# Gated S4 convolution and MLP on one core: the last group of the turn loaded in two parts, its rows reseated

## The chip, the cores and the metric

The kernel runs on one core of one Trainium2 chip. The metric is the device time of the program in microseconds (us): the median of the runs before is 535.32 us (three runs, 534.39 to 537.9). One execution was profiled; it took 536.27 us itself, of which 534.5 us are the span from the first to the last instruction. All times "at" which something happens below are counted from the start of that span.

## The reference

Every token of a sequence of L = 2048 rows and D = 512 columns goes through two branches, which a sigmoid gate mixes.

```
g = sigmoid((x * gate_w).sum(-1, keepdims=True))       # one gate per row
# branch a: S4 convolution, x is [1, 2048, 512], 128 states per column
dt = exp(log_dt)[:, None];  A = A_re + 1j*A_im;  dB = dt * (B_re + 1j*B_im)
P  = exp((dt * A)[:, :, None] * arange(L))
K  = einsum("dn,dnl,dn->dl", C, P, dB).real            # taps, 512 x 2048
y  = irfft(rfft(pad(x^T)) * rfft(pad(K)))[..., :L]     # causal convolution by FFT of 4096
a  = y^T + x * Dskip
# branch b: MLP with F = 1792
h  = gelu(x @ w1 + b1);  b = h @ w2 + b2
return g * a + (1 - g) * b
```

## The kernel before, in words

The kernel has two stages. The first one, `front`, makes the taps K, the first half of the transforms of the signal and of the taps, and almost all of the MLP. Its order on the engines is worked out ahead by a planner from costs and due times. It leaves the MLP's part of the result in the output tensor in DRAM, and the half transforms in the DRAM tensors `tu_d` and `tk_d`. The change does not touch it, apart from a table of constants that it does not use.

The second stage, `conv`, is written out by hand, in the order in which each engine runs it. It works on 32 frequencies n of the outer transform, two at a time in 16 steps s:

- `fetch` and `load_u` bring the half transforms of frequency n back from DRAM (SP's queue), eight frequencies ahead for the taps.
- `signal`, `taps` and `product` do the second half of the forward transforms on TensorE (L1090), copy the taps out on ScalarE (L1098), and multiply on VectorE (L1112 to L1117).
- `inverse` does the first half of the inverse transform on TensorE (L1129), into the PSUM tiles `pa`, one for each frequency: 128 partitions, which stand for 32 values of q, two of i and two of c (c is real or imaginary), by 512 columns.
- `turn` copies `pa` to an SBUF tile `sa` on ScalarE (L1135), and stores it in the DRAM tensor `t4_d` (L1138; the profile calls the tensor t_d). Eight frequencies form a group; there are four groups g. Behind the last store of a group, `turn` loads the group from `t4_d` into the SBUF tile `t3` (L1147; the profile calls the tile t). That is the turn: in `sa` the frequencies lie in different tiles and q lies on the partitions, and in `t3` frequency, i and c lie on the 128 partitions and 32 q by 512 columns lie in a row of 64 KB. One frequency of a group owns four partitions, and a group owns 32.

The first three groups are loaded by the GpSimd queue, in four DMAs of 512 KB, each with 32 rows of 16 KB. The last group, behind frequency 31, is on the path to the end: its last store goes out on ScalarE's queue, and its eight loads of 256 KB, each with 32 rows of 8 KB (four of the 32 q), go out alternately on ScalarE's and SP's queue. Each of the eight waits until all eight stores of the group have landed, so the one that landed last lets them go.

Between the last `inverse` and the first use of `t3`, TensorE works off the remainder of the MLP that `front` put aside for this place (`rest`, L1168 to L1170), and one matmul that keeps it busy (`warm`, L1206).

The final loop over m = 0..7 does the second half of the inverse transform: for m, four of the 32 q of `t3` (4m to 4m+3, on all partitions) are multiplied by the constant `g1t` into two PSUM tiles `pb` (L1218). So pb of m = 0 needs the first load of group 3, m = 1 the second, and so on. Each tile is then multiplied by the gate and added to the MLP's part, on VectorE (L1229), or for five of the sixteen tiles on ScalarE and GpSimd (L1226, L1227), and the result is written to the output: m = 0 and m = 7 in two DMAs of 256 KB (L1231), the others in one of 512 KB (L1233). The program ends when all of them have landed.

`seat(n)` gives the partition of `t3` (and the row of `g1t`) that frequency n takes. Before, a partition is 64 i + 32 c + 4 (n mod 8) + n div 8.

Of the kernel before, what the change touches and what calls it, by code (L numbers as in the profile page):

```python
# [9 lines left out]
F32 = mybir.dt.float32  # L10
# [7 lines left out]
P = 128  # L18
L = 2048
D = 512  # L20
# [50 lines left out]
N_KEEP = 1  # L71
N_PASS = 20
N_LATE = 2

N_ATTIC, N_LOFT, N_TK = 11, 8, 8
N_US = N_ATTIC + N_LOFT
# [2 lines left out]
GROUP = 8  # L79
# [13 lines left out]
def slot_q():  # L93
    return [32 + m if m < 32 else 63 - m for m in range(64)]


def k0_order():
    return [8 * (n % 4) + n // 4 for n in range(32)]


def seat(n):

    return 4 * (n % 8) + n // 8


def constants():


    def om(e4):
        a = 2.0 * np.pi * (np.asarray(e4) % (4 * L)) / (4 * L)  # L110
        return np.cos(a), -np.sin(a)

    k0 = np.arange(32)
    p = np.arange(32)
    q = np.asarray(slot_q())
    k1 = np.arange(64)
    qn = np.arange(64)

    er, ei = om(4 * (64 * np.outer(p, k0) + 16 * p[:, None]))

    c1 = np.concatenate([np.stack([er, ei], 2).reshape(32, 64)] * 4, 0)


    rows = np.zeros((2, 64, 32))
    for n, k in enumerate(k0_order()):
        rows[:, seat(n)] = er.T[k] / L
        rows[:, seat(n) + 32] = ei.T[k] / L
    g1 = rows.reshape(P, 32)

    ko = k0_order()
    f2 = np.zeros((32, 2, 64, 64))
    g2 = np.zeros((32, 64, 64, 2))
    for n, k in enumerate(ko):
        er, ei = om(4 * (q[:, None] * k + 32 * np.outer(q, k1)) + q[:, None])
        f2[n, 0], f2[n, 1] = er, -ei
        er, ei = om(4 * (qn[None] * k + 32 * np.outer(k1, qn)) + qn[None])
        g2[n, :, :, 0], g2[n, :, :, 1] = er, -ei
    f2 = f2.reshape(8, 4, P, 64).transpose(0, 2, 1, 3).reshape(8, P, 256)  # L140
    g2 = g2.reshape(8, 2, P, P).transpose(0, 2, 1, 3).reshape(8, P, 256)
    c2 = np.concatenate([f2, g2], 2)
    return (
        np.ascontiguousarray(c1, dtype=np.float32),
        np.ascontiguousarray(g1, dtype=np.float32),
        np.ascontiguousarray(c2, dtype=np.float32),
    )
# [142 lines left out]
def gated_mix(  # L290
# [18 lines left out]
    nc = tc.nc  # L309

    cp = ctx.enter_context(tc.tile_pool(name="cp", bufs=1))
    dr = ctx.enter_context(tc.tile_pool(name="dr", bufs=1, space=DRAM))

    dt_d = dr.tile([1, D], F32, name="dt_d")
    t4_d = dr.tile([4, 2, 2, GROUP, 32, D], F32, name="t4_d")
    tu_d = dr.tile([2, 32, 2, 64, D // 2], F32, name="tu_d")
    tk_d = dr.tile([2, 32, 2, 64, D // UW, 64], F32, name="tk_d")

# [28 lines left out]
    def front(pool, psum, keep, attic, loft):  # L347
# [554 lines left out]
        def output(u, s, fs, t):  # L902

            b = u % NSB
            if u == 2 * NSB - 1 and s >= NT - N_LATE:
                for f in fs:
# [142 lines left out]
    def conv(pool, ps, late, attic, loft):  # L1049
# [81 lines left out]
        def turn(s):  # L1131

            for n in (2 * s, 2 * s + 1):
                sa = sas[n % 6]
                nc.scalar.copy(sa, pas.pop(n))  # L1135
                g, k = divmod(n, GROUP)
                on = nc.sync if n < 31 else nc.scalar
                on.dma_start(t4_d[g, :, :, k].rearrange("i c q d -> q (i c) d"), sa)  # L1138
                if k < GROUP - 1:
                    continue  # L1140
                rows = t4_d[g].rearrange("i c k q d -> (i c k) q d")


                w = 8 if n < 31 else 4
                for h in range(0, 32, w):
                    on = nc.gpsimd if n < 31 else (nc.scalar, nc.sync)[h // w % 2]
                    on.dma_start(t3[g:P:4, h : h + w], rows[:, h : h + w])  # L1147

        accs, mos = {}, {}

# [22 lines left out]
        for n in range(N_TK):  # L1173
            fetch(n)
            if n == 1:
                t3 = pool.tile([P, 32, D], F32, name="t3", bufs=1)
# [6 lines left out]
        for s in range(16):  # L1183

            for n in range(2 * s + N_TK + (2 if s else 0), min(2 * s + N_TK + 4, 32)):
                fetch(n)
            for n in range(2 * s + N_US, min(2 * s + N_US + 2, 32)):
                load_u(us[n % N_US], n)
            product(s)
            if s + 1 < 16:  # L1190
                signal(s + 1)
            if s + 2 < 16:
                if s % 2 == 0:
                    matrices(s // 2 + 1)
                taps(s + 2)
            if s == 15:
                rest(N_REST)
            inverse(s)
            turn(s)
            if 6 <= s < 14:  # L1200
                dense(s - 6)
# [3 lines left out]
        for _ in range(N_KEEP):  # L1205
            nc.tensor.matmul(warm[0:64], mats[7][0][1][:, 3], zs[0], start=True, stop=True)  # L1206
        for s in range(N_LATE):
            z = mos[7][:, s]
            a = accs[NT - N_LATE + s]
            nc.vector.scalar_tensor_tensor(z, a, gate[:, 1, 14 + s : 15 + s], z, ALU.mult, ALU.add)  # L1210

        for m in range(8):
            tag, n = ("pa", 2) if m % 3 == 2 else ("pu", 4)
# [7 lines left out]
            for i in range(2):  # L1221
                t = 2 * m + i
                z, g = mos[m][:, i], gate[:, 0, t : t + 1]
# [32 lines left out]
def layout(inputs):  # L1256
# [12 lines left out]
    prm = np.stack([np.asarray(inputs[n])[order].T for n in names], 1)  # L1269
    w1 = np.asarray(inputs["B_w1"]).reshape(4, P, NF, P).transpose(2, 1, 0, 3).reshape(NF, P, D)  # L1270
    c1, g1, c2 = constants()
    return {
        "xl": xl,
# [38 lines left out]
```

## Time and profile before

| what | value |
|---|---|
| median of the runs | 535.32 us |
| the profiled execution's own time | 536.27 us |
| its span | 534.5 us |
| TensorE matmul busy | 503.5 us (94%), 4426 instructions |
| VectorE busy | 426.6 us (80%) |
| ScalarE busy | 358.6 us (67%) |
| GpSimd busy | 47.3 us (9%) |
| DMA | 108.61 MB, mean 203 GB/s |
| first to last instruction that the change touches | the turn's stores from 429.3 us, the last loads' issue at 514.8 us |

The table's busy shares are means over stages with different limits. The stage that the change touches is the last tenth of the span, and it has to be read by itself: the chain of waits tells which work ended last there, the table of windows tells how busy the 16 DMA engines and the four compute engines were in each stretch, and the list of DMA issues tells how long a transfer took from its issue to its landing.

### The profile page before, as it was taken

To read this page: it belongs to the slowest core of one execution; us is meant where nothing else is said; L and a number is where in the kernel's file an instruction comes from. 1 tells how busy PE (TensorE), PEld (TensorE's weight loads), DVE (VectorE), ACT (ScalarE), POOL (GpSimd) and SP (SyncE) were. 2 spreads that over 40 slices of the span, in tenths; PEclk is the share of its full clock that TensorE was granted. 3 is DMA by queue.
4 is the path that set the end of the run, shared out by engine and by line. 5 is a ranking of instruction groups with operands and counts; after the bars stand their busy time and mean duration, and the time that the engine had idled before them with its cause. 6 is when DMAs were issued, how large, how long until landed. Compare 5 with 4: busy or idle time off the path is not lost.

```text
span 534.5 us, 11251 instructions
## 1 busy us (share of the span) xinstructions
PE 503.5 (94%) x4426; PEld 352.9 (66%) x4426; DVE 426.6 (80%) x790; ACT 358.6 (67%) x547; POOL 47.3 (9%) x90
## 2 busy tenths in 40 slices
PE   7979999999999799999999999999994899999992
PEld 4757778788777577888788877788783433333360
DVE  5998999989999789999998899997610567666533
ACT  5799887699966898976388968566532454555311
POOL 1000000000000020003110311041001001010103
PEclk9989999999999899999999999999998799999997
DMA  8998923462299269438820547075409979999877
GB/s 254 371 340 308 340 86 117 140 221 66 80 289 304 84 215 279 149 99 219 195 42 2 159 86 152 1 178 89 131 6 217 306 252 312 359 414 385 311 282 288
DMA packets 90837, 108.61 MB, mean 203 GB/s; under 512 B 39056, under 2 KB 58576, under 8 KB 90144
## 3 DMA queue, kind: packets, MB, share of 16 engines
q1 hardware_dynamic: 82944, 87.67, 49.7%
q0 software_dynamic: 7360, 18.65, 14.2%
q10 hardware_dynamic: 480, 1.57, 0.8%
q8 instruction: 35, 0.57, 0.5%
q14 instruction: 18, 0.15, 0.1%
HBM read 62.25 MB, written 45.62 MB: 202 GB/s over the span
## 4 chain that ended last, share of the span: by engine, by line
PE 66%; DVE 11%; DMA 9%; ACT 5%; issue 4%; SPq 2%; POOL 1%; POOLq 0%; DVEq 0%; ACTq 0%
PE pz L706 9%; PE ph L870 7%; PE ph L871 7%; PE ph L872 7%; PE acc L916 6%; PE acc L917 6%; PE acc L918 6%; PE p2k L1090 6%; PE p2u L1090 6%; PE pa L1129 5%; DMA out_dram<-io 2%; PE pz L424 2%; DMA cc<-in_c_dram 1%; DVE y L670 1%; SPq L745 1%
## 5 line engine op out<-in xcount | busy, mean ns | idle before, releaser
L870 PE MATMUL ph<-xh,wh 128*128 128x512 f32 x224 | 90.1, 402 | 0.0
L916 PE MATMUL acc<-wh,hh 128*128 128x512 f32 x210 | 86.0, 410 | 3.4 <-ACT acc L922 2.8
L871 PE MATMUL ph<-xlo,wh 128*128 128x512 f32 x224 | 87.9, 392 | 0.5 <-DVE xlo L804 0.5
L872 PE MATMUL ph<-xh,wl 128*128 128x512 f32 x224 | 87.6, 391 | 0.0
L917 PE MATMUL acc<-wl,hh 128*128 128x512 f32 x210 | 82.7, 394 | 0.0
L918 PE MATMUL acc<-wh,hl 128*128 128x512 f32 x210 | 82.6, 393 | 0.0
L706 PE MATMUL pz<-y,xc 128*32 128x64 f32 x2048 | 61.8, 290 | 5.2 <-ACT attic L450 5.2
L889 ACT ACTIVATE io<-ph,b1t 128x512 f32<-128x512 f32 x56 | 38.6, 689 | 39.2 <-PE ph L872 30.4
L706 PEld LDWEIGHTS pz<-y,xc 128*32 128x32 f32 x2048 | 57.1, 136 | 11.5 <-ACT attic L450 6.1
L898 DVE TENSOR_TENSOR hl<-io,hh 128x512 fp32r<-128x512 f32 x56 | 38.4, 685 | 24.6 <-ACT hh L890 24.6
L916 PEld LDWEIGHTS acc<-wh,hh 128*128 128x128 f32 x210 | 39.7, 189 | 20.1 <-issue 7.1
L870 PEld LDWEIGHTS ph<-xh,wh 128*128 128x128 f32 x224 | 42.3, 189 | 13.8 <-issue 3.8
L871 PEld LDWEIGHTS ph<-xlo,wh 128*128 128x128 f32 x224 | 42.4, 189 | 9.5 <-DVE xlo L804 0.9
L872 PEld LDWEIGHTS ph<-xh,wl 128*128 128x128 f32 x224 | 42.3, 189 | 9.2
L918 PEld LDWEIGHTS acc<-wh,hl 128*128 128x128 f32 x210 | 39.8, 190 | 8.8
L670 DVE TENSOR_TENSOR y<-y,ea 128x64 f32<-128x64 f32 (+4 forms) x80 | 45.2, 565 | 0.4
L1112 DVE TENSOR_TENSOR v<-p2u,k 128x512 f32<-128x512 f32 x16 | 11.1, 691 | 42.5 <-ACT sa L1135 25.3
L917 PEld LDWEIGHTS acc<-wl,hh 128*128 128x128 f32 x210 | 40.0, 190 | 7.5
L515 DVE TENSOR_TENSOR loft<-xc,zz 128x256 f32<-128x256 f32 (+2 forms) x48 | 37.1, 772 | 0.6 <-ACT xc L641 0.5
L516 DVE TENSOR_TENSOR loft<-xc,zz 128x256 f32<-128x256 f32 (+2 forms) x48 | 37.0, 771 | 0.0
L683 DVE TENSOR_TENSOR y<-y,loft 128x2048 f32<-128x2048 f32 x16 | 36.6, 2284 | 0.6 <-ACT loft L633 0.5
L890 ACT CAST hh<-io 128x512 fp32r<-128x512 f32 x56 | 34.8, 622 | 1.8
(139 smaller groups left out, 842.1 us busy)
## 6 DMA issues: line engine op xcount, KB each, us to landing
tu_d<-attic SPq DMA_DIRECT2D x16, 512.0 KB, 4.9
tk_d<-sk SPq DMA_DIRECT2D x16, 512.0 KB, 6.9
tk<-tk_d SPq DMA_DIRECT2D x32, 256.0 KB, 4.9
t_d<-sa SPq DMA_DIRECT2D x31, 256.0 KB, 5.3
t<-t_d POOLq DMA_DIRECT2D x12, 512.0 KB, 7.0
attic<-tu_d SPq DMA_DIRECT2D x22, 256.0 KB, 4.4
attic<-in_xt_dram SPq DMA_DIRECT2D x16, 256.0 KB, 4.1
attic<-in_xl_dram SPq DMA_DIRECT2D x16, 256.0 KB, 4.3
```

The source lines that it names most:

```text
L515: vec(2 * m, lambda: vv.tensor_mul(t, a, br), due, [ka, *kb], [kt])
L670: nc.vector.tensor_mul(both(n, 64 - 3 * n, n), both(0, 64 - n, n), an)
L706: nc.tensor.matmul(pk[32 * j : 32 * j + 32, gg // 4, gg % 4], x[:, r, :, ch], y[:, r, :, ch], start=(r == 0), stop=(r == 1), skip_group_ch ...
L870: nc.tensor.matmul(phs[q], h, xh[d], start=(d == 0), stop=False)
L871: nc.tensor.matmul(phs[q], h, xlo[d], start=False, stop=False)
L872: nc.tensor.matmul(phs[q], lo, xh[d], start=False, stop=(d == 3))
L889: nc.scalar.activation(g, phs[q], AF.Gelu_apprx_tanh, bias=b1t[:, c : c + 1])
L898: SB, lambda: nc.vector.tensor_sub(hl[f], g, hh[f].bitcast(F32)), t + D_LO,
L916: nc.tensor.matmul(a, h, wh[1][f], start=(f == 0 and u >= NSB), stop=False, skip_group_check=True)
L917: nc.tensor.matmul(a, h, wl[1][f], start=False, stop=False, skip_group_check=True)
L918: nc.tensor.matmul(a, l, wh[1][f], start=False, stop=(f == FH - 1), skip_group_check=True)
L1090: nc.tensor.matmul(out[64 * i : 64 * i + 64], w, x, start=True, stop=True)
```

## The change

There are three edits. First, the seats: the partition of a frequency becomes 64 i + 8 (n mod 8) + 4 c + n div 8, so that the frequencies of a group lie one behind the other, and the DRAM tensor `t4_d` is laid out in the same order, with one frequency's 256 KB in one block. `g1t` follows, with the same numbers in other rows. Second, the loads of groups 0 to 2 go by i: two halves of the 32 q for each of two i, each DMA with 16 rows of 32 KB, 512 KB as before. Third, the last group: its last store goes out on SP's queue like the others, and behind it come the loads in two parts. The first part is six frequencies (24 to 29), all 32 q at once, one DMA for each i, 12 rows of 64 KB, both on SP's queue. They wait for the stores of these six frequencies alone. The second part is the frequencies 30 and 31, and waits for the last store: for each i one DMA with 4 rows of 16 KB (q 0 to 7) and one with 4 rows of 48 KB (q 8 to 31), i = 0 on SP's queue and i = 1 on ScalarE's.

```diff
+N_PART = 6
 ...
 def seat(n):
-    return 4 * (n % 8) + n // 8
+    return 8 * (n % 8) + n // 8
 ...
         rows[:, seat(n)] = er.T[k] / L
-        rows[:, seat(n) + 32] = ei.T[k] / L
+        rows[:, seat(n) + 4] = ei.T[k] / L
 ...
-    t4_d = dr.tile([4, 2, 2, GROUP, 32, D], F32, name="t4_d")
+    t4_d = dr.tile([4, GROUP, 2, 2, 32, D], F32, name="t4_d")
 ...
                 g, k = divmod(n, GROUP)
-                on = nc.sync if n < 31 else nc.scalar
-                on.dma_start(t4_d[g, :, :, k].rearrange("i c q d -> q (i c) d"), sa)
-                if k < GROUP - 1:
+                nc.sync.dma_start(t4_d[g, k].rearrange("i c q d -> q (i c) d"), sa)
+                if n < 31 and k < GROUP - 1:
                     continue
-                rows = t4_d[g].rearrange("i c k q d -> (i c k) q d")
-
-
-                w = 8 if n < 31 else 4
-                for h in range(0, 32, w):
-                    on = nc.gpsimd if n < 31 else (nc.scalar, nc.sync)[h // w % 2]
-                    on.dma_start(t3[g:P:4, h : h + w], rows[:, h : h + w])
+                for lo, hi in ((0, N_PART), (N_PART, GROUP)) if n == 31 else ((0, GROUP),):
+                    cuts = (0, 8, 32) if lo else (0, 32) if n == 31 else (0, 16, 32)
+                    for h0, h1 in zip(cuts, cuts[1:]):
+                        for i in range(2):
+                            at = 64 * i + g
+                            to = t3[at + 8 * lo : 64 * i + 8 * hi : 4, h0:h1]
+                            on = nc.gpsimd if n < 31 else (nc.sync, nc.scalar)[i if lo else 0]
+                            on.dma_start(to, t4_d[g, lo:hi, i, :, h0:h1])
```

## The prediction

> **What bounds the kernel now.** The page's mean shares say little here: TensorE is busy for 94% of the span, but the change touches only the last 27 us. I read first the chain of waits from 507 us on (start, length, what).
>
> ```profile
> 507.36 0.60 ACT sa L1135
> 507.96 0.02 issue
> 507.98 4.67 DMA t_d<-sa
> 512.65 0.02 issue
> 512.66 0.03 SPq L1147
> 512.69 0.04 issue
> 512.73 0.50 SPq L1147
> ...
> 514.54 5.36 DMA t<-t_d
> ```
>
> The last store leaves at 507.98 and lands at 512.65; the eight loads are issued behind that. So the wait that the change shortens is real, and is on the chain. Next, the windows: length, busy time of PE, PEld, DVE, ACT and POOL, granted clock, DMA share, GB/s.
>
> ```profile
> 507.00:511.20 4.20, 4.20 (x19) 3.41 (x19) 0.00 (x0) 0.95 (x2) 0.00 (x0) 1.00 0.98 380
> 511.20:514.00 2.80, 2.80 (x14) 2.33 (x13) 0.75 (x1) 0.00 (x0) 0.00 (x0) 1.00 0.03 10
> 514.00:520.30 6.30, 6.30 (x74) 2.81 (x74) 2.70 (x4) 0.92 (x2) 0.32 (x1) 1.00 0.95 343
> 516.00:517.00 1.00, 1.00 (x4) 0.19 (x2) 0.73 (x1) 0.00 (x0) 0.00 (x0) 1.00 1.04 434
> 526.00:531.40 5.40, 0.00 (x0) 0.00 (x0) 0.08 (x1) 0.00 (x0) 0.21 (x1) 0.79 1.00 388
> 531.40:534.50 3.10, 0.00 (x0) 0.00 (x0) 0.00 (x0) 0.00 (x0) 0.00 (x0) 0.50 0.04 15
> ```
>
> The DMA engines are full up to 511.2, idle for 2.8 us, and then near full up to 531.4; 3.1 us of closing follow. It looks as if 2.8 us could be filled. The timeline of the engines that use the loads says otherwise (start, length; in brackets the idle time before):
>
> ```profile
> 515.85 0.39 PE L1170 MATMUL acc<-wh,hl 128*128 128x512 f32 x1
> 516.17 1.07 PE L1206 MATMUL warm<-z,f 128*64 128x512 f32 x2
> 517.17 7.16 PE L1218 MATMUL pb<-t,g1t 64*32 64x512 f32 x128
> 518.35 2.72 DVE L1229 SCALAR_TENSOR_TENSOR loft<-pb,gate,loft 128x512 f32<-128x512 f32 x4 [1.32 <-PE pb L1218]
> 520.99 5.09 DVE L1229 SCALAR_TENSOR_TENSOR attic<-pb,gate,attic 128x512 f32<-128x512 f32 x7
> 519.13 1.04 SPq L1231 DMA_DIRECT2D out_dram<-loft  x2
> 521.29 1.57 SPq L1233 DMA_DIRECT2D out_dram<-loft  x2
> 526.84 1.10 SPq L1231 DMA_DIRECT2D out_dram<-attic  x1
> ```
>
> TensorE has other matmuls until 517.2, and the first pb follows at once. From 518.35 to 526.1 VectorE has no gap: once started, it never waits for a load. The first output is issued at 519.13, and the 4.19 MB of output at 388 GB/s are 10.8 us of transfer, begun some 1.3 us behind the issue (loads: issue 512.73, DMA full from 514.0): 520.4 + 10.8 = 531.2, which is the 531.4 of the window. So the loads are already covered by the MLP's remainder on TensorE. With pb unable to start before 517.2, loads that came earlier would save at most some 0.2 us. A gain over 1% (5.4 us, about what a measurement of this kernel can tell from no change) is excluded by these rows.
>
> **The change part by part.** *Seats, `t4_d` and `g1t`.* The store still writes 128 pieces of 2 KB, and pb reads the same number of partitions: nothing. *Loads of groups 0 to 2*: the same 512 KB in four DMAs, in 16 rows instead of 32.
>
> ```profile
> 495.93 2.04 POOL L1147 DMA_DIRECT2D t<-t_d  x4 [18.75 <-DMA attic<-out_dram]
> 505.30 0.55 SPq L1138 DMA_DIRECT2D t_d<-sa  x1
> t_d<-sa SPq DMA_DIRECT2D x1, 256.0 KB, 5.5
> t_d<-sa ACTq DMA_DIRECT2D x1, 256.0 KB, 4.7
> t<-t_d POOLq DMA_DIRECT2D x12, 512.0 KB, 7.0
> ```
>
> The third of these groups is issued at 495.93, lands some 7 us later, and is not read before 517.2. That 14 us slack hides it; without it the cost would be a longer landing, 0 to 2 us on the stores beside it. I take nothing.
>
> *The last store on SP* is queued behind the one of frequency 30 there, which ends its issue at about 508.0, so it leaves some 0.05 us later than from ScalarE, and the same backlog drains at 511.2: nothing.
>
> *The six-frequency part* waits for the store of frequency 29, issued at 505.30 with 5.5 us to landing: 510.8. Its two DMAs are issued at 510.85 and 511.4, 1.9 us before the first load now, first bytes 1.3 us on, at 512.15. SP has nothing else queued behind it until the output, so the wait itself holds up only the second part. *The second part* is issued behind the last landing, 512.65, as now: two DMAs on SP, two on ScalarE, which is idle then.
>
> What decides is over how many of the 16 engines these DMAs are spread. The queue rows of the page for ScalarE's queue, and its issues:
>
> ```profile
> q10 hardware_dynamic: 480, 1.57, 0.8%
> t<-t_d ACTq DMA_DIRECT2D x4, 256.0 KB, 5.2
> out_dram<-attic ACTq DMA_DIRECT2D x1, 256.0 KB, 6.0
> ```
>
> ScalarE's queue carries six DMAs: four loads of 32 rows, one store and one output of 128 pieces. That is 128 + 256 = 384 pieces, and 480 packets; the 96 left over are 6 x 16, one closing packet on each engine for each DMA. So a row of up to 8 KB went as one packet, and all 16 engines took part; 16 divides both 32 and 128. The new loads have 12 and 4 rows of up to 64 KB. If a row stays one packet, at most 12 and 4 engines can work. On the DRAM side the outermost count is smaller still: `t4_d[g, lo:hi, i]` steps over six and two frequencies, with c inside and not joinable, since i lies between. If every engine gets whole steps of both sides, it is six and two engines.
>
> Bounds, with the 434 / (16 x 1.04) = 26.1 GB/s of one engine in the window 516 to 517. Upper number of engines, all sixteen: 1.57 + 0.52 MB go as fast as now. Middle, 12 and 4: the four common engines carry 256 KB, 10.0 us. Lower, six and two, always the same first ones: the six-part puts 256 KB on each of six engines (10.0 us), and the four DMAs of the second part put another 256 KB on each of two of them: 524 KB (512 KB in units of 1024), 20.1 us. I take the lower, because every DMA of the page fits a deal in equal shares on both sides, and six and two are the largest numbers that allow it. No row has such a count, so the other ends stay in the range.
>
> [...]
>
> The sum: first bytes at 512.15, plus 20.1 = 532.3, plus a landing of about 1.2 (the last store's data end at 511.2 and its landing is at 512.65) = 533.5. The pieces q 0 to 7 are somewhat earlier, so m = 0 and 1 are computed and sent by then. m = 2 needs the last piece: pb at 533.5, TensorE some 0.9, ScalarE and GpSimd one step each before the first of six outputs is issued.
>
> ```profile
> L1229 DVE SCALAR_TENSOR_TENSOR attic<-pb,gate,attic 128x512 f32<-128x512 f32 x7 | 4.9, 744 | 0.2
> L1227 POOL TENSOR_TENSOR attic<-attic,sa 128x512 f32<-128x512 f32 x3 | 3.7, 1269 | 0.0
> L1226 ACT ACTIVATE sa<-pb,gate 128x512 f32<-128x512 f32 x5 | 3.4, 688 | 12.8 <-PE pb L1218 12.8
> ```
>
> 533.5 + 0.9 + 0.69 + 1.27 = 536.4, first bytes 537.7, six outputs of 524 KB at 388 GB/s 8.1 us: 545.8, closing 3.1: 548.9. VectorE's eight steps of 0.74 end near 540.6, inside that. So the span grows by 14.4 us.
>
> TensorE now idles for some 12 us behind `warm`, and a row shows what that brings:
>
> ```profile
> 415.57 2.54 PE L1090 MATMUL p2k<-tk,cc 128*64 128x512 f32 x4 [9.22 <-ACT f L1075]
> 414.00:418.00 4.00, 2.43 (x6) 1.36 (x8) 0.00 (x0) 1.33 (x4) 0.00 (x0) 0.50 0.98 326
> 418.00:422.00 4.00, 4.00 (x17) 2.39 (x15) 1.15 (x2) 1.17 (x2) 0.00 (x0) 0.77 1.07 365
> ```
>
> After 9.2 us idle the clock stood at 0.50 and came back within 4 us. The pb of m = 0 and 1 would pay most of it while the rest is still loading; between 0 and 2 us remain for m = 2, and I take 0.
>
> The profiled execution took 536.27 us with a span of 534.5; its 1.8 us around the span stay. Against the median of the runs, 535.3, the forecast is 535.3 + 14.4 = 549.7 us.
>
> **The rivals.**
>
> *More engines, 12 and 4* (one for each row). For it: a row is all that a packet must keep together. Against it: the source's six and two. The four engines end at 522.2, with the landing 523.4; the pieces for m = 0 come 1.9 us earlier (one 48 KB packet fewer), 521.5, against 517.2 now. First output 1.96 us on, as now from 517.17 to 519.13: 523.5; first bytes 524.8, plus 10.8 and 3.1 = 538.7 in the span, 4.2 us more: 539.5 us, within 1%.
>
> *Six and two engines, but not the same ones* (each DMA begins elsewhere): then the longest engine has 10.0 us, everything has landed at 523.4, m = 0 starts with it, and the sum is 523.4 + 1.96 + 1.3 + 10.8 + 3.1 = 540.6 in the span: 541.4 us.
>
> *Not slower: all sixteen take part*, because a row of 64 KB is cut into smaller packets that are dealt out. The first part ends at 512.15 + 3.9 = 516.1, the first pieces of the second at 516.4, landed at 517.6; pb starts 0.4 us later than now at worst, and the outputs follow as now: 535.3, within 0.5. This case decides as soon as the first pieces land before 517.2. For it speaks that nothing in the trace says a row can't be cut; against it that rows up to 8 KB were not.
>
> *The change doesn't do what it says*: the six-part still waits for the last store, if the wait is kept for the whole of `t4_d` and not by frequency. Then it is issued 1.9 us later, and with the forecast's engines the time is 551.6 us; with sixteen the first pieces land 1.9 us later than in the case before, 519.5, 2.3 us behind pb now: 537.6.
>
> **How the numbers follow.** Forecast (six and two, the same engines) 0.66; the same with a late wait 0.06; other engines 0.06; 12 and 4 0.09; all sixteen 0.13. The range runs from 539 to 554: it holds the first three cases with their clock and landing bounds, and half of the fourth, about 0.8 in all. Slower by over 1% are the first three cases, 0.78. Within 1% are the last two, less a remainder: 0.20. Faster by over 1% needs pb earlier than TensorE allows: 0.02.
>
> **What would show it.** ScalarE's queue would have 4 + 4 + 128 pieces and 2 + 2 + 16 closing packets, 156 in all, and 184 if all sixteen engines close. The six-part's issue should stand near 510.85 on SP. The DMA share between 514 and 521 should lie near 6/16, and near 2/16 up to 532, with TensorE idle from 517.2 to about 529 and the clock at 0.5 there. The time to landing of the 768 KB loads should be over 10 us. The prediction is wrong if the DMA share stays near 1 behind 512, or if pb starts before 520.

## The result, and the profile after

The changed kernel takes 569.11 us (median of four runs, 564.57 to 570.55) against 536.47 us before: a ratio of 1.0596, 95% interval 1.0554 to 1.0637. That is 32.6 us slower, where 14.4 were forecast, and above the range of 539 to 554. The profiled execution is the fastest of the four: it took 564.57 us, with a span of 562.8, 28.3 us more than before.

Of the page of the changed kernel, the span, the row of ScalarE's queue (packets, MB, share of 16 engines), and the row of the loads of groups 0 to 2 (count, KB each, median us to landing):

```profile
span 562.8 us, 11246 instructions
...
q10 hardware_dynamic: 156, 0.52, 0.2%
...
t<-t_d POOLq DMA_DIRECT2D x12, 512.0 KB, 11.0
```

156 packets is what the prediction named for six and two engines: 4 + 4 rows, 128 pieces of output, and 2 + 2 + 16 closing packets. So the DMAs of the second part ran on two engines each. But the loads of groups 0 to 2, which were costed at nothing, now take 11.0 us to land instead of 7.0. The chain of waits of the changed kernel from 475 us on (start, length, what) shows where both end up:

```profile
475.90 16.75 DMA tk<-tk_d
...
492.79 3.88 PE p2k L1091 x8
...
509.19 10.98 DMA t_d<-sa
520.17 0.02 issue
520.18 0.03 SPq L1148
520.21 0.03 issue
520.24 0.90 SPq L1148
...
522.07 22.33 DMA t<-t_d
544.40 0.14 issue
544.53 2.27 PE pb L1219 x16
```

There are three new stretches. A load of taps takes 16.75 us to land, and TensorE waits for it; before, no such load is on the chain in this stretch. The store of frequency 29 leaves at 509.19 instead of 505.30 and takes 10.98 us instead of 5.5, so that the six-frequency part is issued at 520.24 and not at 510.85. And the loads of the last group take until 544.40. The windows of the changed kernel (length, busy PE, PEld, DVE, ACT, POOL, granted clock, DMA share, GB/s):

```profile
480.00:490.00 10.00, 9.40 (x42) 2.92 (x40) 6.36 (x12) 3.91 (x7) 0.00 (x0) 1.00 1.04 228
490.00:500.00 10.00, 7.21 (x24) 2.81 (x26) 2.63 (x5) 3.57 (x8) 0.00 (x0) 0.83 1.00 357
...
525.00:530.00 5.00, 0.00 (x0) 0.00 (x0) 0.00 (x0) 0.00 (x0) 0.00 (x0) 0.50 0.36 105
...
540.00:545.00 5.00, 0.47 (x8) 0.42 (x16) 0.00 (x0) 0.00 (x0) 0.00 (x0) 0.50 0.12 52
```

From 525 the share of the DMA engines is 0.36, about 6/16, and later 0.12, 2/16. In the first of the two, however, a busy engine moves 105 / (16 x 0.36) = 18.2 GB/s, and in the second 52 / (16 x 0.12) = 27. Between 480 and 490 it is worse: all 16 engines look busy and move 228 GB/s, where they moved 390 before:

```profile
480.00:490.00 10.00, 10.00 (x46) 3.10 (x44) 6.69 (x12) 4.86 (x11) 0.00 (x0) 1.00 1.03 390
```

### The profile page after: what moved, and what is told of

It reads as the page before. It is cut to its first block, busy times and chain, and to the rows that moved or that the text cites. A ratio compares the mean times of both kernels' runs of the same rounds, so it can differ in the third digit from the quotient of the medians.

```text
span 562.8 us, 11246 instructions
## 1 busy us (share of the span) xinstructions
PE 505.4 (90%) x4426; PEld 352.9 (63%) x4426; DVE 427.2 (76%) x790; ACT 358.5 (64%) x547; POOL 47.8 (9%) x90
## 4 chain that ended last, share of the span: by engine, by line
PE 61%; DMA 18%; ACT 8%; DVE 5%; issue 4%; SPq 1%; POOL 1%; DVEq 0%; POOLq 0%; ACTq 0%
PE pz L707 8%; PE ph L871 7%; PE acc L917 7%; PE ph L872 6%; PE ph L873 6%; PE acc L918 6%; PE acc L919 6%; PE p2k L1091 4%; DMA tk<-tk_d 4%; DMA t<-t_d 4%; PE p2u L1091 4%; PE pa L1130 3%; DMA t_d<-sa 3%; DMA out_dram<-io 3%; DMA tk_d<-sk 3%
## 5 line engine op out<-in xcount | busy, mean ns | idle before, releaser
L890 ACT ACTIVATE io<-ph,b1t 128x512 f32<-128x512 f32 x56 | 38.6, 690 | 38.1 <-PE ph L873 26.1
L871 PEld LDWEIGHTS ph<-xh,wh 128*128 128x128 f32 x224 | 42.1, 188 | 13.4 <-issue 3.7
```

What stands on the lines that cost most here:

```text
L871: nc.tensor.matmul(phs[q], h, xh[d], start=(d == 0), stop=False)
L890: nc.scalar.activation(g, phs[q], AF.Gelu_apprx_tanh, bias=b1t[:, c : c + 1])
```

## The experiments

The questions were: how much each of the two places costs; what slows down the rows; and whether the wait that the change avoids was worth anything.

**Which place costs what.** Two runs keep one half of the change each. The seats are set group by group, so that the other half stays exactly as before.

```diff
 # groups 0-2 as before, last group as changed
-    return 8 * (n % 8) + n // 8
+    return 4 * k + g if g < 3 else 8 * k + g        # c: + 32 if g < 3 else + 4
+    if g < 3:  for h in range(0, 32, 8): nc.gpsimd.dma_start(t3[g:P:4, h : h + 8], rows[:, h : h + 8])
```

> Groups 0 to 2 get back their seats, their layout in DRAM and their loads of 32 rows of 16 KB; the last group stays as in the changed kernel. Theory: the changed kernel loses at two places, some 9 us because groups 0 to 2 are loaded in large rows by few engines, which holds up the taps' loads and the stores, and the rest because the last group is loaded by six and two engines. Then the six-part is issued near 511 instead of 520 and the time is 555 to 560 us. Rival: the first loads cost nothing, as the prediction took it, and the whole loss is the last group's: then the time stays at 569.

```diff
 # groups 0-2 as changed, last group as before
+    return 8 * k + g if g < 3 else 4 * k + g        # c: + 4 if g < 3 else + 32
+    last group: for h in range(0, 32, 4): (nc.scalar, nc.sync)[h // 4 % 2].dma_start(t3[g:P:4, h : h + 4], rows[:, h : h + 4])
```

> The counterpart: groups 0 to 2 as in the changed kernel, the last group with the seats, layout, queues and eight loads of before. Theory of two places: 543 to 548 us, and what this run and the one with the old first groups lose against before adds up to the changed kernel's loss. Rival (the first groups cost nothing): 536.

With the first groups as before: 558.11 us, ratio 1.0407 (1.0371 to 1.0444), 21.8 us slower than before. With the last group as before: 551.39 us, ratio 1.0283 (1.0246 to 1.0321), 15.1 us slower. Both places cost, the first groups more than the 9 us expected. The two add up to 36.9 us, 4.3 more than the change as a whole. The traces show where they overlap: in the changed kernel pb waits long for the last group's loads, so what TensorE has lost before that counts only as far as it delays these loads (TensorE's timeline; in brackets the idle time before):

```profile
520.07 1.07 PE L1207 MATMUL warm<-z,f 128*64 128x512 f32 x2
544.53 3.42 PE L1219 MATMUL pb<-t,g1t 64*32 64x512 f32 x32 [23.39 <-DMA t<-t_d]
```

With the last group as before, `warm` starts at 528.33, 12.2 us later than in the kernel before, and pb waits only 2.80 us for a load. In the first of these runs SP issues the six-part at 511.14, in the second a load of taps again takes 17 us (the timeline of SP, then the chain, of the one and of the other):

```profile
511.14 4.26 SPq L1162 DMA_DIRECT2D t<-t_d  x4
```

```profile
482.69 17.12 DMA tk<-tk_d
```

**What slows the rows: the source?** In the changed kernel the frequencies of a DMA lie 256 KB apart in DRAM.

```diff
-    t4_d = dr.tile([4, GROUP, 2, 2, 32, D], F32, name="t4_d")
+    t4p = dr.tile([4, GROUP, 4 * 32 * D + 1024], F32, name="t4_d")
+    t4_d = t4p[:, :, : 4 * 32 * D].rearrange("g k (i c q d) -> g k i c q d", i=2, c=2, q=32)
```

> The changed kernel with 4 KB of padding behind each frequency's 256 KB in DRAM, nothing else. The 32 KB rows took 2.0 to 2.4 us each and the first 64 KB rows 3.4 to 5.2, against 0.61 for 16 KB before, so about half speed. If the equal steps of 256 KB in DRAM are the cause (engines that read in step hit the same part of it), the rows go at full speed, the taps' loads are held up less and the time falls by 5 to 12 us, to 557 to 564. If the cause is the number of engines or the write side, it stays at 569.

It took 568.31 us, ratio 1.0603 (1.0564 to 1.0641): no change against 569.11. The steps in DRAM are not the cause.

**The length of a row?** Once in the changed kernel, and once in the kernel before.

```diff
-   else (0, 16, 32)
+   else (0, 8, 16, 24, 32)      # changed kernel, groups 0-2: rows of 16 KB
```

> The changed kernel with the loads of groups 0 to 2 cut into rows of 16 KB (eight DMAs of 256 KB a group instead of four of 512), on the same 16 rows each. If the length of a row is what holds up the other queue on the same engine, the part lost in the first groups goes and the time is 555 to 560 us, as with the old first groups. If the few engines or the half speed are the cause, the taps still wait and it stays within 3 us of 569.

```diff
-                w = 8 if n < 31 else 4
+                w = 16 if n < 31 else 4      # kernel before, groups 0-2: 32 rows of 32 KB
```

> The kernel before with one edit: groups 0 to 2 are loaded in two DMAs of 32 rows of 32 KB (1 MB each) instead of four of 32 rows of 16 KB. All 16 engines take part and the rows lie as before, only the row is as long as in the changed kernel. Theory: the length of a row is harmless by itself, a group's load still takes 7 to 9 us (230 to 290 GB/s) and the time is 535 to 538 us. Rival (large rows hold up the smaller pieces of the other queue on the same engine): the taps' loads wait and the time is 542 to 552 us.

Shorter rows do not help the changed kernel: 566.69 us, ratio 1.0586 (1.0538 to 1.0634). Longer rows do not hurt the kernel before: 536.36 us, ratio 1.0022 (0.9997 to 1.0048). So the length of a row, up to 32 KB, is not the cause.

**The write side?** The rows of the last group, on as many engines and with the same bytes, but on the old seats, where the six rows of one DMA lie 4 partitions apart:

```diff
+                        for i in range(2):
+                            for c in range(2):
+                                at = 64 * i + 32 * c + g
+                                to = t3[at + 4 * lo : min(at + 4 * hi, P) : 4, h0:h1]
+                                on.dma_start(to, t4_d[g, i, c, lo:hi, h0:h1])
```

> The kernel before with the last group in two parts, six frequencies and two, cut and queued as in the changed kernel, but on the old seats, where c steps 32 partitions: so one DMA for each i and c, six or two rows each. Engines and bytes for each engine are those of the run with the old first groups (six and two; 256 KB and again 256 KB on the first two), where the 64 KB rows took 3.7 us in the mean instead of the 2.5 of a full engine, and of the first six rows two took 2.9 and 3.4 and four 4.3 to 5.2. Theory of the write side: rows whose partitions differ by a multiple of 32 within one half of 64 share a way into SBUF, and in the changed kernel engines 0 and 4, and 1 and 5, always write such rows at the same time; here the six rows of one DMA all differ. Then a 64 KB row takes 2.5 us, all rows are in 20 to 21 us behind the first byte instead of 26.6, and the time is 550 to 554 us. [...] Rival (few engines, or the source, are slow in themselves): 3.7 us a row and 557 to 560 us.

It took 548.65 us, ratio 1.0224 (1.019 to 1.0259), 9.5 us less than with the seats of the change. The windows in which the six engines load, first in the run with the changed seats, then here (columns as above):

```profile
514.00:519.00 5.00, 3.61 (x14) 2.02 (x12) 0.75 (x1) 0.00 (x0) 0.00 (x0) 1.00 0.34 92
```

```profile
514.00:519.00 5.00, 3.11 (x12) 1.60 (x10) 0.75 (x1) 0.00 (x0) 0.00 (x0) 1.00 0.38 164
...
525.00:532.00 7.00, 2.17 (x24) 1.12 (x32) 0.02 (x1) 0.00 (x0) 0.00 (x0) 0.50 0.12 51
```

A busy engine moves 92 / (16 x 0.34) = 16.9 GB/s in the one and 164 / (16 x 0.38) = 27.0 in the other. The partitions differ, and with them the number of DMAs and the order in DRAM (steps of 64 KB here, 256 KB in the change). In the changed kernel the rows of a DMA lie at 64 i + 4 j + 3, j = 0 to 11. If each of the six engines takes two neighbouring rows, the first and the fifth write j = 0 and 8 first, 32 partitions apart, and then j = 1 and 9; the second and the sixth do likewise, and the two in the middle meet nobody. The single rows in the trace of the changed kernel agree: of the first six, four took 4.3 to 5.2 us and two 2.9 and 3.4. Here no two rows of a DMA are 32 apart, the first six took 2.4 to 3.2 us, and the next six 2.42 each. The order in DRAM is an unlikely cause: padding it changed nothing (568.31 us), and the sixteen sharing rows below are slow with steps of 64 KB (13.9 GB/s of a busy engine). That rows 32 apart share a way into SBUF is the author's theory, and so is which engine takes which row, for the trace does not name the engines; the 16.9 and 27.0 GB/s of these two runs agree with it.

For groups 0 to 2, the same in both directions: eight rows 4 apart (with rows of 32 KB and of 16 KB), and sixteen rows 8 apart for sixteen engines.

```diff
 # kernel before, groups 0-2 (the 16 KB run: h in range(0, 32, 8), h : h + 8)
+                    for h in (0, 16):
+                        for i in range(2):
+                            for c in range(2):
+                                at = 64 * i + 32 * c + g
+                                nc.gpsimd.dma_start(t3[at : min(at + 32, P) : 4, h : h + 16], t4_d[g, i, c, :, h : h + 16])
```

> The kernel before with one edit: groups 0 to 2 are loaded in rows of 32 KB by eight engines as in the changed kernel, but with one DMA for each i and c (8 rows, 256 KB), so that the rows of one DMA lie on partitions 4 apart over 32 and none share a way in. Theory of the write side: the rows take 1.2 us each instead of 2.3 and the time is 536 to 541 us. Rival (eight engines for a DMA are too few, or large rows hold up the other queue): 2.3 us a row, the taps' loads wait, 547 to 553 us, as in the run with the changed first groups alone (551.4).

> The kernel before with one edit: groups 0 to 2 in rows of 16 KB as before, but one DMA for each i, c and quarter of the q: eight rows, 128 KB, sixteen DMAs a group. No two rows of a DMA share a way in. With rows of 32 KB in the same deal (554.3 us) only eight rows were ever under way at a time, at full speed, and a group's load took 12 to 15 us. Theory: eight engines at a time are the cause, whatever the row: 11 to 15 us a group and 548 to 555 us. Rival (the cause was the long row together with few engines): 7 to 10 us a group and 535 to 541 us.

```diff
 # groups 0-2: seat 8 * (k % 4) + 4 * (k // 4) + g, c at + 32; last group as before
+                    for h in (0, 16):
+                        for f in range(2):
+                            rows = t4_d[g, f].rearrange("i c k q d -> (i c k) q d")
+                            nc.gpsimd.dma_start(t3[4 * f + g : P : 8, h : h + 16], rows[:, h : h + 16])
```

> The other way round: groups 0 to 2 in rows of 32 KB, but each DMA has 16 rows from four frequencies, both i and both c, one row for each of all 16 engines; its seats lie 8 partitions apart over all 128, so two rows of a DMA always share a way in (they differ by 32). The last group is as before. Theory of the write side: the rows take about 2.3 us though all 16 engines work, the DMA moves some 215 GB/s, and the time is 546 to 553 us. Rival (few engines are the cause): 1.2 us a row and 536 to 541 us.

The eight clean rows: 554.33 us, ratio 1.0326 (1.0292 to 1.036), and with 16 KB 552.92 us, ratio 1.0312 (1.0271 to 1.0352). The sixteen rows that share: 546.37 us, ratio 1.0186 (1.0147 to 1.0225). The first did not come back to before, against the expectation; the second is as bad as the theory of few engines says; the third is slow though 13.6 engines are busy with it. (In the third, the first of a group's four DMAs needs four frequencies only, and leaves 9 to 11 us ahead of the other three, so less is left for the stretch below.) The rows of GpSimd's queue in a stretch within the load of group 1 tell why: packets, MB, and the share of 16 engines' time. Before (478 to 485 us):

```profile
q0 software_dynamic: 187, 2.03, 69.8%
```

Kernel before with 32 rows of 32 KB (478 to 485):

```profile
q0 software_dynamic: 82, 1.67, 62.3%
```

Changed kernel (480 to 491):

```profile
q0 software_dynamic: 179, 2.00, 83.8%
```

Eight clean rows of 32 KB (485 to 496), then of 16 KB (485 to 496):

```profile
q0 software_dynamic: 218, 1.84, 44.9%
```

```profile
q0 software_dynamic: 421, 1.74, 41.3%
```

Sixteen rows that share (483 to 491):

```profile
q0 software_dynamic: 91, 1.51, 84.8%
```

| groups 0 to 2 loaded in | GB/s of the load | engines busy with it | GB/s of a busy engine | taps' load beside it, us to landing | time against before |
|---|---|---|---|---|---|
| 32 rows of 16 KB (before) | 290 | 11.2 | 26.0 | 10.1 | 1 |
| 32 rows of 32 KB | 239 | 10.0 | 23.9 | 10.7 | 1.0022 |
| 16 rows of 32 KB, steps of 8 frequencies (changed) | 182 | 13.4 | 13.6 | 15.4 | 1.0283 |
| 8 clean rows of 32 KB | 167 | 7.2 | 23.3 | 15.1 | 1.0326 |
| 8 clean rows of 16 KB | 158 | 6.6 | 24.0 | 15.7 | 1.0312 |
| 16 sharing rows of 32 KB | 189 | 13.6 | 13.9 | 12.2 | 1.0186 |

(MB over the length of the stretch; share times 16; the one over the other; the median of the taps' loads issued in the stretch; the last column is each run's ratio, for the changed form that of the run with the last group as before.) Two things take the same toll. Each of the sixteen sharing rows has others of its DMA 32 partitions away, and a busy engine moves 13.9 GB/s instead of 26.0. And where no rows of a DMA are 32 apart, the DMAs of eight rows kept only 7.2 and 6.6 engines busy. Either way the load of a group moves 160 to 190 GB/s instead of 290. The changed kernel's loads look like the first kind: 13.4 engines are busy, where the expectations took eight as an estimate, and at half speed. Clean rows on 7.2 and 6.6 engines brought nothing here, and neither did rows 32 apart on 13.6.

One thing stays open. The 32 rows of the kernel before lie 32 apart too, and yet a busy engine moves 26.0 GB/s, in the load of group 1 from the first row on (0.61 to 1.05 us for each row of 16 KB). If each of the 16 engines takes two of the 32 rows, and the two that lie 32 apart go to the same engine, they never meet; but this is a guess, for the trace does not name the engines, and no run here tests it.

**How that reaches TensorE.** In all of the slower runs of the table but the last, a load of taps, issued on SP's queue about when a group's load is issued, stands on the chain of waits with 15 to 18 us, up to about the end of that load, and TensorE waits for it. The taps' loads beside the faster loads of the kernel before (10.1 us) and of the run with 32 KB rows (10.7 us) do not stand on the chain there. In the run with sixteen sharing rows another load on the same queue is late, that of the constants, for which ScalarE waits (its waits between 440 and 520 us: in total, times, longest):

```profile
ACT f L1082 <- DMA cc<-in_c_dram: 4.2, 1, 4.2
```

One run was meant to show whether the taps' load is held by the load as such, by spreading a group's four loads over the following steps:

```diff
+            if pending:
+                nc.gpsimd.tensor_copy(junk, v[0][:, :1])
+                nc.gpsimd.dma_start(*pending.pop(0))
```

> As the run with the changed first groups alone (551.4 us: groups 0 to 2 as in the changed kernel, last group as before), but the four loads of a group are not issued together: one goes out in each of the four following steps, behind a one-column copy on GpSimd that waits for that step's product. Bytes, rows, engines and shared ways are the same. There, one taps' load came in only 17 us after its issue, some 1 us behind the last row of a group's load (11 to 13 us for 2 MB at 150 to 190 GB/s), and TensorE stood still for it. Theory: the taps' load is held up for as long as a group's load runs, so spread out it is held up for one DMA (3 us) and the lead of four pairs hides that: the gaps in TensorE between 450 and 510 go and the time is 536 to 541 us. Rival (the loss is the DMA capacity that slow rows use up, however they are spread): 547 to 553 us.

It took 553.24 us, ratio 1.0329 (1.0292 to 1.0365). GpSimd's timeline of this run around group 1, and the chain:

```profile
482.18 0.53 POOL L1130 DMA_DIRECT2D t<-t_d  x1 [14.97 <-DMA tk<-tk_d]
...
482.83 0.53 POOL L1130 DMA_DIRECT2D t<-t_d  x1
...
483.48 0.53 POOL L1130 DMA_DIRECT2D t<-t_d  x1
```

```profile
481.69 18.20 DMA tk<-tk_d
```

The first load of the group waited 15 us, and by then the next two were due, so three went out within 1.3 us. They were not spread, and the run decides nothing between the two theories. That the taps' loads on SP's queue take longer beside a slower group's load, 10.1 us beside 290 GB/s and 15.1 to 15.7 beside 158 to 182, is what the table shows; why is left open.

**Was the wait worth anything?** The kernel before, with the last eight loads reading rows of group 2, so that its result leaves the last group out:

```diff
+                    src = rows if n < 31 else t4_d[2].rearrange("i c k q d -> (i c k) q d")
-                    on.dma_start(t3[g:P:4, h : h + w], rows[:, h : h + w])
+                    on.dma_start(t3[g:P:4, h : h + w], src[:, h : h + w])
```

> The kernel before, but the eight loads of the last group read the rows of group 2, which have long landed, so they wait for no store; the last group's data are left out of the result. It shows what the wait can be worth at all. The prediction says that the tail does not hang on the loads, because TensorE has other matmuls until 517.2: between 0 and 0.5 us faster. Rival: the idle 2.8 us of the DMA engines behind the last store are on the path; then 2 to 3 us faster.

It took 535.69 us, ratio 0.9993 (0.9973 to 1.0012). The timelines of SP and TensorE in this run, and its window behind the last store:

```profile
507.14 3.50 SPq L1148 DMA_DIRECT2D t<-t_d  x4
```

```profile
515.21 1.07 PE L1207 MATMUL warm<-z,f 128*64 128x512 f32 x2
516.21 7.17 PE L1219 MATMUL pb<-t,g1t 64*32 64x512 f32 x128
```

```profile
511.00:514.00 3.00, 3.00 (x15) 2.45 (x15) 0.31 (x1) 0.00 (x0) 0.00 (x0) 1.00 0.98 366
```

The loads leave 5.6 us earlier than before, and the 2.8 us in which the DMA engines idled are gone (a share of 0.98), but pb still starts right behind `warm`. The wait that the change shortens was worth nothing.

**The idea with all engines.** Two parts of four frequencies, 16 rows for 16 engines each:

```diff
+                for f in range(2):
+                    rows = t5_d[f].rearrange("i c k q d -> (i c k) q d")
+                    for h in range(0, 32, 8):
+                        on = nc.sync if f == 0 else (nc.scalar, nc.sync)[h // 8 % 2]
+                        on.dma_start(t3[4 * f + g : P : 8, h : h + 8], rows[:, h : h + 8])
```

> The idea of the change with all 16 engines: groups 0 to 2 as before; the last group in two parts of four frequencies, each part seated so that its four frequencies, both i and both c are 16 rows 8 partitions apart, one for each engine. The first part (four DMAs of 256 KB, rows of 16 KB) goes out on SP behind the last store and waits for the first four stores alone; the second part (the same four cuts, on ScalarE's and SP's queue) waits for the last store. Theory: few engines and shared ways are the whole loss and the wait was worth nothing, as the run without any wait showed (ratio 0.9993), so the time is that of before, between 0.5 us less and 2 us more, the latter because two rows of a DMA share a way in. Rival (loading in parts has a cost of its own, or the early loads delay the last store): 3 to 6 us more. Second rival (the early half does shorten the tail): 1 to 3 us less.

It took 539.19 us, ratio 1.0075 (1.0048 to 1.0102): 3.1 us slower than before, and more than the 2 us that were allowed for. Its window, TensorE's timeline, and the load that pb waits for, from the chain:

```profile
511.00:516.00 5.00, 4.45 (x18) 2.71 (x16) 0.75 (x1) 0.00 (x0) 0.00 (x0) 1.00 1.00 216
```

```profile
519.11 8.80 PE L1230 MATMUL pb<-t,g1t 64*32 64x512 f32 x128 [3.66 <-DMA t<-t_d]
```

```profile
511.64 7.33 DMA t<-t_d
```

All 16 engines are busy and move 216 GB/s, 13.5 each: the 16 rows lie 8 apart over 128 partitions, so each has another 32 away. A load of the second part, issued behind the last store, takes 7.33 us to land instead of the 5.2 of before, and pb waits 3.66 us. Half of the group is loaded early, and pb still starts later than before.

## Why the prediction was right or wrong

**The loads are covered, nothing can be gained:** right. Without any wait the ratio is 0.9993.

**Six and two engines, always the same ones:** right. 156 packets on ScalarE's queue, a DMA share of 0.36 and then 0.12. That the two are two of the six, the term that gives the 20.1 us, was an estimate: the trace does not name the engines, and no run shows which they are. What the runs showed in its place is the end of the loads. In the run with the old first groups and clean rows, which is the forecast's own case, the sum holds: the six-part is issued at 511.17 (forecast 510.85), the two engines work up to 532.9 (532.3), and the time is 548.65 us (549.7). The span of the profiled execution, the slowest of the four at 551.25 us, is 549.5 (548.9). One small slip is in the sum: the landing of "about 1.2" us is 1.45 by the two times given for it.

**The six-part waits for the first six stores alone:** right by 511.14 and 511.17 in the two runs with the old first groups; in the changed kernel itself it is 520.24, since the store of frequency 29 leaves 3.9 us late and takes 5.5 us longer to land.

**26.1 GB/s of one engine:** the first mis-sized term. It came from a window in which 32 rows went to 16 engines. With 12 rows on the new seats, a busy engine of the six-part moved 16.9 to 18.2 GB/s; in the run with clean rows it moves 27.0, and that run is 9.5 us faster than the one with the old first groups and the new seats. The seats were taken as "nothing" because the store writes the same pieces and pb reads as many partitions; that a busy engine could move 16.9 GB/s on the one kind and 27.0 on the other was not seen.

**"Loads of groups 0 to 2: ... I take nothing":** the step that failed. Its reason, a slack of 14 us, looked only at who reads `t3`, and its bound allowed the stores beside such a load 0 to 2 us, where the store of frequency 29 took 5.5 us longer. How fast a busy engine would move the new rows was not asked for these loads. A group's load slowed from 290 to 182 GB/s, not because engines were missing (13.4 were busy, 11.2 before) but because each moved 13.6 GB/s instead of 26.0; a taps' load beside it took 17.12 us, TensorE waited for it, and the stores before the last group came late. Alone this costs 15.1 us, ratio 1.0283. Had the sum had this and the cost of the seats, 14.4 + 9.5 + 15.1 = 39 us, it would have been above the measured 32.6, since what the two places cost overlaps.

**The clock:** in the clean run pb took 10.14 us from 529.83 on, waits for its later pieces included, with a granted clock of 0.50 from 525 to 532, against 7.16 before the change. The bound of 0 to 2 us on the end was not measured by itself.

**The rivals.** All sixteen engines, and 12 and 4, are excluded by the packets and the shares, and others than the same ones by the loads' end at 532.9, where that rival has all landed at 523.4. That the change doesn't do what it says is excluded by 511.14: the last store of that run lands at 514.04.

## What to carry to other kernels

When a DMA is reshaped, count its rows and the outermost steps of each side, and ask how many engines they will keep busy: here, on SP's and ScalarE's queues, 12 rows from six frequencies kept six engines busy (a share of 0.36), and four rows from two kept two (0.12). Then list the partitions of the rows that are under way at the same time: with rows 32 apart among the same 64 partitions a busy engine moved 13.5 to 13.9 GB/s in three layouts here, and 26.0 in the kernel before. Ask both for each DMA that the edit touches, those off the path too: the first groups alone cost 15.1 us. And before any of this, test whether a wait is worth something by letting the transfer read data that landed long ago: one run showed here that there was nothing to win.

## What the runs showed of the hardware that was not expected

- Rows of a DMA that lie 32 partitions apart, within the same 64, were slow: 13.5 to 13.9 GB/s of a busy engine in three layouts, on GpSimd's queue and on SP's and ScalarE's, 16.9 where, by the estimate from the seats, four of six engines meet another, 27.0 where no rows of a DMA are 32 apart. In two of the three layouts (13.9 and 13.5) the DMA has rows 64 apart too, and the rate is a half of the 26.0 to 27.0, not a quarter. The kernel before has rows 32 apart as well and moved 26.0; why is open.
- DMAs of eight rows on GpSimd's queue, issued one behind the other, had 7.2 and 6.6 rows under way in the mean, and by the single rows in the trace never more than eight, so the load of a group by such DMAs did not fill the 16 engines. Whether they were the same eight engines can't be read from the trace.
- The load of 256 KB on SP's queue that stands on the chain of waits beside a slow load of group 1 took 16.5 to 18.2 us, whether the group's rows were of 16 or 32 KB, and whether a busy engine moved 13.6 GB/s or 23.3 and 24.0: 16.75 us in the changed kernel, 17.12 with the last group as before, 17.89 and 16.48 with eight clean rows of 32 and of 16 KB, 18.20 in the run that tried to spread them. Beside the load of the kernel before it took 10.1, and beside the sixteen sharing rows, a quarter of which leave earlier, 12.2.
